# Loading and turning a mixer's input in halves, behind the last two hidden tiles of the mixer before it

## The chip, the cores and the metric

The kernel runs on one core of one Trainium2 chip. The metric is the device time of one execution in microseconds; the number compared is the median over several runs. TensorE (PE, its weight loads are listed as PEld), VectorE (DVE), ScalarE (ACT) and GpSimd (POOL) each work through their own list of instructions in order. SyncE (SP) issues the DMAs, also in order, so a DMA that must wait holds up every DMA behind it in that list.

## The reference

Linear attention per head, followed by a mixer over tokens and channels; everything is float32.

```
phi(x):  proj = x @ w_phi;  proj -= max(|proj|)           # per token, 64 -> 128
         return concat(exp(proj), exp(-proj))             # 256 features
q_p, k_p = phi(q), phi(k)                                 # q, k, v: 8 batches, 8 heads, 576 tokens, 64
kv, z = k_p^T @ v, sum over tokens of k_p
attn  = (q_p @ kv) / (q_p . z + 1e-6)                     # x: 8 x 576 x 512 after the heads are joined
u   = x + V^T (U^T x)          # over tokens, rank 32
out = u + relu(u @ w_ch1) @ w_ch2                         # 512 -> 2048 -> 512
```

The weights of the mixer (U, V, w_ch1, w_ch2) arrive as float64 and are converted on the chip.

## The kernel before, in words

**Attention.** Work goes through 32 pairs of heads, `Pair(b, j)` with batch b = 0 to 7 and j = 0 to 3. At a time there are three pairs in flight: `cur`, `nxt` and `far`. A pair's steps are `transposes` (k and q brought to features-on-partitions as tiles `T`), `s_project_k0` and `s_project_k1` (PSUM tiles `pkt` and `pk`, features `kp`), `s_project_q0` and `q1` (`pq`, `qp`), `s_kv` (`kv_ps`, copied by VectorE to `kv`), and `s_out` (`xpt`, `xp`, then `normalize` on VectorE, whose last multiplication writes `x`). From batch 2 on (`split`), k and q are loaded as 32 x 32 blocks into `raw`, and VectorE turns each block in place (STREAM_TRANSPOSE, line 347) before ScalarE and VectorE split it into a high and a low part.

**Tokens.** `tokens(tk, fill)` runs after the last pair of a batch: `split`, `down` (`pp`, then `pst` by ScalarE and VectorE), `up(t)` for t = 0 to 4 (TensorE writes `vp`, VectorE adds it to `x` or to `xt`, SyncE stores the result to the DRAM buffer `u_dram`). Five tiles cover the 576 tokens; the fifth, of 64 tokens, goes to a ninth row block that is mixed at the very end. `fill` holds the steps of the next batch's first pair, which are put between.

**Mixer.** `Mixer(g, x)` does relu(u @ w1) @ w2 for 512 tokens in 16 hidden tiles: `hidden(f)` is 12 matmuls into `ph`, which ScalarE turns into `h_hi` and VectorE into `h_lo` (line 667); `add(f)` is 12 matmuls that accumulate `h_hi` and `h_lo` times w2 into four PSUM tiles `o`. The right-hand side of `hidden` is `uT_hi` and `uT_lo`, one buffer each. From batch 2 on these come from `y`: `load_blocks` reads `u_dram` back in 32 x 32 blocks with four DMAs, and `turn_blocks(c)` turns a quarter on VectorE (line 653) and splits it (lines 258 and 259). `finish` adds the residual `st` to `o` on VectorE (line 704).

**Order.** The pieces of a mixer wait in the list `todo` (`chunks()`: hidden 0, hidden 1, add 0, hidden 2, add 1, ...). `pace.step()` after each attention step takes pieces from it, so that a mixer of batch b-1 is worked off among the attention steps of batch b. From pair 9 on TensorE's instructions keep the order in which they are written (`in_order`); on the other engines, and in SyncE's list, a scheduler sets the order from its own estimate, except where `tc.issue_after` puts an instruction behind a named one in the order (it adds no wait). At the end of `tokens` all but `HELD` = 4 pieces of the old mixer are emitted, then the new input is turned with two more pieces between, and the last two adds are left for the next steps.

**Names used below.** I call the stretch around the change of mixers a boundary; there are six, at the end of the tokens of batches 2 to 7. PSUM tiles of the tag `at` (`pkt`, `pk`, `pq`, `kv_ps`, `xpt`, `xp`, `vp`, `pp`) share three banks; `ph` has one bank, so `hidden(f + 1)` cannot begin before `h_lo` of tile f has been read out of it (but for the last mixers, which use `at` banks for every second `ph`).

## Time and profile before

| | |
|---|---|
| median of three runs | 1186.46 us (1184.69 to 1186.94) |
| the profiled execution | 1189.84 us, of which the span from first to last instruction is 1188.1 us |
| TensorE matmuls busy | 1130.9 us, 95% of the span, mean granted clock 0.982 |
| VectorE busy | 671.6 us, 57% |
| ScalarE busy | 538.9 us, 45% |
| GpSimd busy | 202.5 us, 17% |
| DMA moved | 110.28 MB, mean 93 GB/s |

Rows of the profile give an engine, a line of kernel.py, an operation, its output and inputs, its duration, and in square brackets the time that the engine stood idle just before it and what ended that wait. SPq is SyncE's list of DMAs: its duration is the time to issue, not the time to land. PEclk is the clock that TensorE was granted, as a share of full speed.

### The profile page before, as it was taken

What the parts mean: (1) busy time and instruction counts of PE and PEld (TensorE: products, weight loads), DVE (VectorE), ACT (ScalarE), POOL (GpSimd) and SP (SyncE); (2) the same over time, 40 slices, a digit from 0 to 9 for tenths busy, and PEclk for the clock granted to TensorE, in tenths of its full rate; (3) what the DMA queues carried; (4) which work ended last, traced back from release to release, by engine and by line L of the source; (5) the groups of instructions that cost most, each with busy time, mean ns of one, the idle gap of its engine ahead of it and who ended that gap; (6) DMA issues with size and microseconds to landing.
All of it is one profiled execution on the core that took longest, in us unless ns stands there. A gap on an engine that the chain in (4) does not pass through costs nothing.

```text
span 1188.1 us, 22127 instructions
## 1 busy us (share of the span) xinstructions
PE 1130.9 (95%) x8841; PEld 932.3 (78%) x8845; DVE 671.6 (57%) x1482; ACT 538.9 (45%) x1151; POOL 202.5 (17%) x154
## 2 busy tenths in 40 slices
PE   7989988999998999899999999899989998999998
PEld 5767866778887888688878888688878877888886
DVE  6567787766666666566657665666666433212111
ACT  6678887545444554254535544355535421111110
POOL 4234355211110111011201111011201200000000
PEclk9998999999999999899999999899999999999999
DMA  5785511332354224532363235323461117410201
GB/s 147 230 258 195 159 49 29 105 102 67 85 104 104 67 58 100 105 81 52 86 121 102 66 84 112 95 59 67 104 118 46 42 68 143 108 54 36 71 1 36
DMA packets 246599, 110.28 MB, mean 93 GB/s; under 512 B 211296, under 2 KB 223840, under 8 KB 246496
## 3 DMA queue, kind: packets, MB, share of 16 engines
q1 hardware_dynamic: 246176, 108.34, 36.5%
q8 instruction: 70, 1.15, 0.4%
q10 hardware_dynamic: 320, 0.52, 0.1%
q14 instruction: 33, 0.27, 0.1%
HBM read 86.80 MB, written 22.02 MB: 92 GB/s over the span
## 4 chain that ended last, share of the span: by engine, by line
PE 69%; DVE 13%; DMA 8%; SPq 4%; ACT 4%; issue 2%; POOL 1%; DVEq 0%; ACTq 0%; POOLq 0%
PE ph L79 26%; PE o L79 25%; PE kv_ps L79 5%; PE xp L79 4%; DMA y<-u_dram 3%; PE pq L79 2%; DMA raw<-in_k_dram 2%; PE pk L79 2%; SPq L647 2%; DVE T L351 1%; PE pp L79 1%; DMA u_dram<-x 1%; SPq L291 1%; DVE w L250 1%; DVE y L653 1%
## 5 line engine op out<-in xcount | busy, mean ns | idle before, releaser
L79 PE MATMUL ph<-uT_hi,w 128*128 128x512 f32 x1152 | 389.1, 399 | 11.2 <-DVE h_lo L667 9.6
L79 PE MATMUL o<-w,h_hi 128*128 128x512 f32 x1152 | 361.2, 399 | 0.4 <-ACT h_hi L666 0.3
L79 PEld LDWEIGHTS ph<-uT_hi,w 128*128 128x128 f32 x1152 | 218.9, 190 | 63.1 <-DVE h_lo L667 14.3
L79 PEld LDWEIGHTS o<-w,h_hi 128*128 128x128 f32 x1152 | 216.5, 191 | 46.4 <-ACT h_hi L666 1.9
L79 PE MATMUL o<-w,h_lo 128*128 128x512 f32 x576 | 226.4, 401 | 15.3 <-DVE h_lo L667 15.3
L79 PE MATMUL ph<-uT_lo,w 128*128 128x512 f32 x576 | 227.5, 395 | 3.5 <-DVE uT_lo L259 3.5
L666 ACT ACTIVATE h_hi<-ph 128x512 fp32r<-128x512 f32 x144 | 85.6, 595 | 294.6 <-PE ph L79 294.3
L667 DVE SCALAR_TENSOR_TENSOR h_lo<-ph,h_hi 128x512 fp32r<-128x512 f32 x144 | 98.9, 687 | 193.7 <-ACT h_hi L666 193.1
L395 POOL PARTITION_ALL_REDUCE qp<-qp x64 | 127.6, 1994 | 261.4 <-ACT qp L394 229.9
L79 PEld LDWEIGHTS o<-w,h_lo 128*128 128x128 f32 x576 | 110.8, 193 | 41.7 <-DVE h_lo L667 17.8
L79 PEld LDWEIGHTS ph<-uT_lo,w 128*128 128x128 f32 x576 | 109.7, 190 | 25.0 <-DVE uT_lo L259 4.2
L395 POOL PARTITION_ALL_REDUCE qp_t<-qp_t x32 | 25.1, 786 | 417.0 <-ACT qp_t L394 417.0
L79 PE MATMUL xp<-kv,qp 128*64 128x65 f32 x2048 | 72.3, 225 | 9.9 <-ACT qp L397 7.7
L351 DVE TENSOR_TENSOR T<-raw,T 64x512 fp32r<-64x512 f32 x96 | 67.7, 705 | 24.2 <-ACT T L350 21.9
L397 ACT ACTIVATE qp<-qp 128x512 f32<-128x512 f32 x64 | 40.3, 629 | 88.7 <-DVE qp L396 88.7
L79 PEld LDWEIGHTS xp<-kv,qp 128*64 128x64 f32 x2048 | 66.0, 140 | 17.3 <-ACT qp L397 9.6
L79 PE MATMUL kv_ps<-vb,kp 128*64 128x65 f32 x2048 | 70.4, 224 | 0.1
L79 PEld LDWEIGHTS kv_ps<-vb,kp 128*64 128x64 f32 x2048 | 64.0, 137 | 7.2 <-issue 2.4
L347 DVE STREAM_TRANSPOSE raw<-raw 128x512 f32<-128x512 f32 x48 | 34.1, 711 | 55.8 <-DMA raw<-in_k_dram 35.7
L385 ACT ACTIVATE kp<-kp 128x512 f32<-128x512 f32 x64 | 40.4, 632 | 54.5 <-DVE kp L382 54.4
L350 ACT CAST T<-raw 64x512 fp32r<-64x512 f32 x96 | 59.2, 617 | 8.7 <-PE pq L79 7.3
L396 DVE TENSOR_TENSOR qp<-qp 128x512 f32<-128x512 f32 x64 | 46.4, 725 | 14.7 <-POOL qp L395 14.5
(119 smaller groups left out, 1267.2 us busy)
## 6 DMA issues: line engine op xcount, KB each, us to landing
w<-kept SPq DMA_DIRECT2D x46, 512.0 KB, 3.8
words<-in_moe_w_ch_dram SPq DMA_DIRECT2D x32, 512.0 KB, 7.8
vb<-in_v_dram SPq DMA_DIRECT2D x64, 128.0 KB, 2.9
u_dram<-x SPq DMA_DIRECT2D x32, 256.0 KB, 2.5
st<-u_dram SPq DMA_DIRECT2D x16, 512.0 KB, 4.5
out_dram<-st SPq DMA_DIRECT2D x32, 256.0 KB, 2.2
y<-u_dram SPq DMA_DIRECT2D x28, 256.0 KB, 5.6
raw<-in_k_dram SPq DMA_DIRECT2D x96, 64.0 KB, 2.4
```

What stands on the lines that cost most here:

```text
L79: ins = nc.tensor.matmul(*args, **kw)
L250: nc.vector.tensor_sub(w[:, 1, :], r, f32(w[:, 0, :]))
L347: nc.vector.transpose(out=x_, in_=x_)
L350: nc.scalar.copy(out=m[here, s, :], in_=x_[here])
L351: nc.vector.tensor_sub(m[there, s, :], x_[here], f32(m[here, s, :]))
L385: nc.scalar.activation(out=kp[:, :, 0:F], in_=kp[:, :, F:2 * F], func=AF.Exp)
L395: nc.gpsimd.partition_all_reduce(qp[:, 0, :], qp[:, 1, :], P, ReduceOp.absmax)
L396: nc.vector.tensor_sub(qp[:, 1, :], qp[:, 1, :], qp[:, 0, :])
L397: nc.scalar.activation(out=qp[:, 0, :], in_=qp[:, 1, :], func=AF.Exp)
L647: nc.sync.dma_start(out=self.y[i * Q:(i + 1) * Q].rearrange("r c (j e) -> r c j e", e=Q), in_=of[i])
L666: on_act = nc.scalar.activation(out=h_hi, in_=ph, func=AF.Relu)
L667: on_dve = nc.vector.scalar_tensor_tensor(out=h_lo, in0=ph, scalar=0.0, in1=f32(h_hi), op0=ALU.max, op1=ALU.subtract)
```

## The change

Four things change.

1. `load_blocks(half)` loads `y` in two halves of 256 tokens, four DMAs each. The first half is loaded after `up(0)` and `up(1)`, the second after `up(2)` and `up(3)`. `turn_blocks(prev)` puts the turns of the first half behind `h_lo` of the old mixer's tile 14 and those of the second half behind `h_lo` of tile 15 in the order; the split into `uT_hi` and `uT_lo` follows the second half, in pieces of the old size. A new `last_chunks` emits all but two pieces of the old mixer, then the turns.
2. In `tokens` from batch 2 on, one pacing step ahead of `up(0)` is left out, so that each `up` stands one or two pieces earlier, and the next batch's second pair has its `s_project_k0` (as the last item of `fill`) ahead of hidden tile 14, rather than behind tile 15.
3. The in-place turns of `raw` stand behind the last multiplication of `normalize` (`divided`).
4. In the last batch, where there is no next pair, two pacing steps are taken ahead of `s_out`; ahead of the mixer of the ninth row block, all but seven pieces are emitted instead of all but four.

```diff
@@ Pair
-            self.raw = []
+            self.raw, self.kp0 = [], None
...
-                    nc.vector.transpose(out=x_, in_=x_)
+                    with tc.issue_after(divided[0].ins):
+                        nc.vector.transpose(out=x_, in_=x_)
@@ normalize
-            nc.vector.tensor_tensor(
+            divided[0] = nc.vector.tensor_tensor(
                 out=xo, in0=xv[:, :, 0:D], in1=den.unsqueeze(2).broadcast_to([np_, m, D]),
                 op=ALU.mult)
@@ Mixer
-        def load_blocks(self):
-            self.y = home.tile([P, NCC, SM], F32, tag="w_late", name=f"y{self.g}")
-            of = u_dram[self.g].rearrange("(j r) (c i e) -> i r c j e", r=Q, i=4, e=Q)
+        def load_blocks(self, half):
+            if half == 0:
+                self.y = home.tile([P, 2, NCC, SM // 2], F32, tag="w_late", name=f"y{self.g}")
+            ts_ = slice(half * SM // 2, (half + 1) * SM // 2)
+            of = u_dram[self.g][ts_].rearrange("(j r) (c i e) -> i r c j e", r=Q, i=4, e=Q)
             for i in range(4):
                 nc.sync.dma_start(
-                    out=self.y[i * Q:(i + 1) * Q].rearrange("r c (j e) -> r c j e", e=Q),
+                    out=self.y[i * Q:(i + 1) * Q, half].rearrange("r c (j e) -> r c j e", e=Q),
                     in_=of[i])
-        def turn_blocks(self, c):
-            y = self.y[:, c, :]
-            nc.vector.transpose(out=y, in_=y)
-            split_t(y, self.uT_hi[:, c, :], self.uT_lo[:, c, :])
+        def turn_blocks(self, prev):
+            for half in range(2):
+                with ExitStack() as order:
+                    for i in prev.parts[NFC - 2 + half]:
+                        order.enter_context(tc.issue_after(i.ins))
+                    for c in range(NCC):
+                        y = self.y[:, half, c, :]
+                        nc.vector.transpose(out=y, in_=y)
+                    if half:
+                        for c in range(NCC):
+                            split_t(self.y[:, :, c, :], *(
+                                a[:, c, :].rearrange("p (h n) -> p h n", h=2)
+                                for a in (self.uT_hi, self.uT_lo)))
@@ hidden
-            self.h[f] = (h_hi, h_lo)
+            self.h[f], self.parts[f] = (h_hi, h_lo), (on_act, on_dve)
@@ tokens
-        pace.step()
+        if not tk.late:
+            pace.step()
         tk.up(0)
         tk.up(1)
         if tk.late:
+            m = Mixer(tk.b, tk.x)
+            m.load_blocks(0)
             pace.step()
             tk.up(2)
             tk.up(3)
-            m = Mixer(tk.b, tk.x)
-            m.load_blocks()
+            m.load_blocks(1)
             pace.step()
             tk.up(NT)
-            mix(len(todo) - HELD)
-            for c in range(NCC):
-                m.turn_blocks(c)
-                mix(c % 2)
-            todo.extend(m.chunks())
+            mix(len(todo) - 5)
+            other()
+            last_chunks(m)
             return
...
+    def last_chunks(m):
+        prev = todo[0][0].__self__
+        mix(len(todo) - 2)
+        m.turn_blocks(prev)
+        todo.extend(m.chunks())
@@ the loop over pairs
-                step(nxt.s_project_k0)
+                if nxt.kp0 is None:
+                    nxt.s_project_k0()
+                pace.step()
                 if nxt.split:
                     pace.step()
+            else:
+                pace.step()
+                pace.step()
...
-                    if not nxt.split:
-                        fill.append(nxt.s_project_q1)
+                    fill.append(
+                        far.s_project_k0 if tk.late else
+                        None if nxt.split else nxt.s_project_q1)
+                    fill = [fn for fn in fill if fn is not None]
@@ the end
-        mix(len(todo) - HELD)
+        mix(len(todo) - 7)
...
-        m.load_blocks()
-        for c in range(NCC):
-            m.turn_blocks(c)
-            mix()
-        todo.extend(m.chunks())
+        m.load_blocks(0)
+        m.load_blocks(1)
+        last_chunks(m)
         mix(len(todo))
```

How that moves the instructions shows at three places of the boundary at the end of batch 2's tokens (and alike at those of batches 3 to 6). First VectorE, from the old mixer's tile 13 to the read-out of its sums (`mk`, `kp`: the key features of the next batch's second pair; `st`: the residual plus `o`). Before:

```order
514 L667 SCALAR_TENSOR_TENSOR h_lo_13_4103<-ph_13_4089,h_hi_13_4102 128x512
515 L347 STREAM_TRANSPOSE raw_3_4507<-raw_3_4507 128x512
516 L617 TENSOR_TENSOR xt_2826<-xt_2826,vp_4_4133 64x512
517 L667 SCALAR_TENSOR_TENSOR h_lo_14_4151<-ph_14_4137,h_hi_14_4150 128x512
518 L653 STREAM_TRANSPOSE y_4116<-y_4116 128x512 x4
519 L380 TENSOR_REDUCE mk_1_t<-pkt_1_4213 128x1
520 L667 SCALAR_TENSOR_TENSOR h_lo_15_4192<-ph_15_4178,h_hi_15_4191 128x512
521 L435 TENSOR_TENSOR kp_1_0_4222<-pk_3_1_4223,kp_1_0_4222 128x2x128
522 L435 TENSOR_TENSOR kp_1_0_4222<-pk_3_1_4228,kp_1_0_4222 128x2x128
523 L259 TENSOR_TENSOR uT_lo_4115<-y_4116,uT_hi_4114 128x512 x3
```

The same engine and place in the changed kernel:

```order
511 L436 TENSOR_TENSOR kp_1_0_4150<-pk_3_1_4151,kp_1_0_4150 128x2x128
512 L436 TENSOR_TENSOR kp_1_0_4150<-pk_3_1_4156,kp_1_0_4150 128x2x128
513 L381 TENSOR_REDUCE mk_1_0_4161<-kp_1_0_4150 128x4
514 L383 TENSOR_TENSOR kp_1_0_4150<-kp_1_0_4150,mk_1_0_4161 128x4x128
515 L680 SCALAR_TENSOR_TENSOR h_lo_14_4180<-ph_14_4166,h_hi_14_4179 128x512
516 L662 STREAM_TRANSPOSE y_4079<-y_4079 128x256 x4
517 L680 SCALAR_TENSOR_TENSOR h_lo_15_4209<-ph_15_4195,h_hi_15_4208 128x512
518 L662 STREAM_TRANSPOSE y_4079<-y_4079 128x256 x4
519 L259 TENSOR_TENSOR uT_lo_4078<-y_4079,uT_hi_4077 128x512 x2
520 L717 TENSOR_TENSOR st_0_4019<-st_0_4019,o_0_3036 128x512
```

Ahead of `h_lo_15` there are now only the four short turns of the first half; the key features have moved in front of `h_lo_14`.

Then VectorE a little later, where the outputs of the next batch's first pair are divided and the new mixer's first `h_lo` follows, in the changed kernel (before, the two turns of `raw` stood elsewhere, and `h_lo_0` came right behind the multiplication):

```order
536 L494 TENSOR_TENSOR x_4228<-xp_3_0_4291,den_0_0_4308 128x4x64
537 L494 TENSOR_TENSOR x_4228<-xp_3_0_4312,den_0_1_4329 128x4x64
538 L348 STREAM_TRANSPOSE raw_2_0_4229<-raw_2_0_4229 128x512
539 L348 STREAM_TRANSPOSE raw_2_1_4234<-raw_2_1_4234 128x512
540 L680 SCALAR_TENSOR_TENSOR h_lo_0_4347<-ph_0_4333,h_hi_0_4346 128x512
```

Two turns now stand between the last multiplication and the new mixer's first `h_lo`.

Last TensorE at the beginning of the boundary, where the second projection of q (`pq`) precedes the first two `up` tiles (`vp`) and add 11 of the old mixer (`o`); - is before, + the changed kernel:

```order
 L79 MATMUL pq_3_0_4060<-T_3_0_3663,w_hl 128x512 x2
+L79 MATMUL vp_0_4069<-pst_3368,v_all 128x512
+L79 MATMUL vp_1_4073<-pst_3368,v_all 128x512
 L79 MATMUL o_0_3036<-w_11_2231,h_hi_11_3907 128x512 x2
 L79 MATMUL o_0_3036<-w_11_2231,h_lo_11_3908 128x512
@@ -825,17 +827,16 @@
 L79 MATMUL o_3_3039<-w_11_2231,h_hi_11_3907 128x512 x2
 L79 MATMUL o_3_3039<-w_11_2231,h_lo_11_3908 128x512
-L79 MATMUL vp_0_4081<-pst_3368,v_all 128x512
-L79 MATMUL vp_1_4085<-pst_3368,v_all 128x512
```

The two `vp` matmuls have moved from behind the twelve of add 11 to right behind `pq`. In SyncE's list the four loads of `y` have become two groups of four, the first ahead of the last stores of `u_dram`, the second behind them and behind four of the eight loads of `raw`. In the last batch the outputs of the last pair (`xpt`, `xp`) have moved on TensorE from between hidden 9 and add 8 to between hidden 10 and add 9, and `pp` there is followed by `vp` at once, where hidden 11 stood between.

More of the change, by code (lines that the diff above doesn't have):

```diff
@@ L262, in tile_kernel @@
     SPLIT, Q, H = 2, 32, P // 2
-    tails = {}
+    tails, divided = {}, [None]
     class Pair:
@@ L627, in __init__ @@
             self.uT_lo = moe.tile([P, NCC, 512], F32R, tag="uT_lo", name=f"uT_lo{g}")
-            self.o, self.h, self.res = None, {}, None
+            self.o, self.h, self.parts, self.res = None, {}, {}, None
         def transposes(self, t):
```

## The prediction

> **What bounds the kernel now.** I read the page's busy shares first, then what TensorE waited for, then TensorE, VectorE and SyncE in order of time around one boundary, and at last the granted clock in ten microseconds around each boundary.
>
> ```profile
> PE 1130.9 (95%) x8841; PEld 932.3 (78%) x8845; DVE 671.6 (57%) x1482; ACT 538.9 (45%) x1151; POOL 202.5 (17%) x154
> ...
> PE o L79 <- DVE h_lo L667: 15.3, 6, 3.5
> PE ph L79 <- DVE h_lo L667: 9.6, 10, 2.6
> ...
> DVE y L653 <- DMA y<-u_dram: 45.5, 7, 7.4
> ```
>
> TensorE is the bound: 1130.9 of 1188.1 us. The columns of the waits are total, count and longest. So a change of order can win back what TensorE stands idle, and the clock that it loses by that. Few long waits make most of it, and they are for `h_lo`, which VectorE makes. Why VectorE is late shows at the boundary of batch 3 (TensorE first, then VectorE, then SyncE):
>
> ```profile
> 489.64 0.61 PE L79 MATMUL o<-w,h_hi 128*128 128x512 f32 x2
> 493.75 0.80 PE L79 MATMUL o<-w,h_lo 128*128 128x512 f32 x1 [3.50 <-DVE h_lo L667]
> ...
> 481.58 0.69 DVE L667 SCALAR_TENSOR_TENSOR h_lo<-ph,h_hi 128x512 fp32r<-128x512 f32 x1 [2.05 <-ACT h_hi L666]
> 489.66 2.49 DVE L653 STREAM_TRANSPOSE y<-y 128x512 f32<-128x512 f32 x4 [7.38 <-DMA y<-u_dram]
> 493.00 0.69 DVE L667 SCALAR_TENSOR_TENSOR h_lo<-ph,h_hi 128x512 fp32r<-128x512 f32 x1
> 494.27 1.89 DVE L259 TENSOR_TENSOR uT_lo<-y,uT_hi 128x512 fp32r<-128x512 f32 x3
> 498.07 1.88 DVE L704 TENSOR_TENSOR st<-st,o 128x512 f32<-128x512 f32 x3
> 502.15 0.76 DVE L493 TENSOR_TENSOR x<-xp,den 128x256 f32<-128x256 f32 x2
> 504.81 0.69 DVE L667 SCALAR_TENSOR_TENSOR h_lo<-ph,h_hi 128x512 fp32r<-128x512 f32 x1 [1.91 <-ACT h_hi L666]
> ...
> 476.67 0.94 SPq L620 DMA_DIRECT2D u_dram<-x  x2
> 479.46 6.62 SPq L647 DMA_DIRECT2D y<-u_dram  x4
> 486.18 1.30 SPq L620 DMA_DIRECT2D u_dram<-xt  x1
> ```
>
> VectorE stands 7.38 us in front of the turns of `y`, whose loads were issued at 479.46 and had landed at 489.66; the last `h_lo` of the old mixer is queued behind them, and TensorE waits 3.50 us for it. The other boundaries read alike; at the last one the wait is booked on `ph` (2.64, below). What the wait costs beyond itself shows in the granted clock (PEclk, third from the end of a row):
>
> ```profile
> 364.00:374.00 10.00, 8.64 (x99) 6.87 (x100) 9.78 (x27) 3.18 (x7) 0.00 (x0) 1.00 0.33 121
> 493.00:503.00 10.00, 9.25 (x90) 7.49 (x91) 9.68 (x26) 1.88 (x4) 0.00 (x0) 0.67 0.28 105
> 622.00:632.00 10.00, 9.93 (x100) 8.12 (x100) 8.99 (x26) 2.43 (x6) 0.00 (x0) 0.83 0.29 107
> 750.00:760.00 10.00, 10.00 (x94) 8.03 (x95) 8.92 (x25) 1.88 (x4) 0.00 (x0) 0.72 0.29 107
> 878.00:888.00 10.00, 9.63 (x98) 8.00 (x99) 9.29 (x26) 2.32 (x6) 0.00 (x0) 0.83 0.29 107
> 997.00:1007.00 10.00, 8.79 (x29) 6.55 (x30) 4.05 (x8) 2.68 (x5) 0.00 (x0) 0.83 0.11 43
> 957.00:967.00 10.00, 7.38 (x57) 6.05 (x52) 4.85 (x17) 2.89 (x7) 0.00 (x0) 0.83 0.03 9
> ```
>
> Five of six boundaries run at 0.67 to 0.83 of full speed for the ten microseconds after the wait. The seventh row is the last pair of batch 7, where TensorE waits for q's features.
>
> **What the change takes away.** (a) The turns leave their place in front of `h_lo`. The `o` group's six waits are 15.3 us, and the row of 997.82 below adds 2.64: 17.9 us.
>
> ```profile
> 997.82 0.77 PE L79 MATMUL ph<-uT_hi,w 128*128 128x512 f32 x1 [2.64 <-DVE h_lo L667]
> 364.62 0.50 PE L79 MATMUL o<-w,h_lo 128*128 128x512 f32 x1 [2.78 <-DVE h_lo L667]
> 622.07 0.52 PE L79 MATMUL o<-w,h_lo 128*128 128x512 f32 x1 [2.54 <-DVE h_lo L667]
> ...
> 477.90 0.50 PE L79 MATMUL ph<-uT_hi,w 128*128 128x512 f32 x1 [1.31 <-DVE h_lo L667]
> 607.15 0.50 PE L79 MATMUL ph<-uT_hi,w 128*128 128x512 f32 x1 [0.28 <-DVE h_lo L667]
> 863.37 0.50 PE L79 MATMUL ph<-uT_hi,w 128*128 128x512 f32 x1 [0.37 <-DVE h_lo L667]
> ...
> 959.43 0.34 PE L79 MATMUL xp<-kv,qp 128*64 128x65 f32 x4 [2.29 <-ACT qp L397]
> 960.09 1.61 PE L79 MATMUL xp<-kv,qp 128*64 128x65 f32 x28 [0.33 <-ACT qp L398]
> ```
>
> (b) The clock behind those waits. Ten microseconds times one minus the clock is 3.3, 1.7, 2.8, 1.7 and 1.7 us; at the boundary of batch 3 some 0.4 of it falls into the wait itself. 10.8 us. (c) The three waits at 477.90, 607.15 and 863.37, where a turn of `raw` that waits for its DMA stands ahead of `h_lo`: 2.0 us. (d) In the last batch hidden 10 and add 8 now run while q's features are made; twelve matmuls of either kind are 2.7 us by the chain of waits:
>
> ```profile
> 508.69 2.74 PE o L79 x12
> ```
>
> So the waits of 2.29 and 0.33 go, and the clock of the seventh row, 1.7: 4.3 us. Sum 35.0 us.
>
> Of the clock the Trainium skill says, in "TensorE: Matmul & The Clock Gate", section "HAM oscillation — how this bites in real kernels", that idle gaps longer than about 3.4 us are to be avoided. By that sentence alone the shorter waits here would cost no clock. The trace does not agree: 2.54 us of idle at 622.07 brought a clock of 0.83, though 2.78 at 364.62 brought none.
>
> **What it adds.** Three prices, and two that I set to nothing. (e) The first two `vp` come right behind `pq`. The second needs the bank of `kv_ps`, which VectorE must have copied out:
>
> ```profile
> 466.54 0.73 PE L79 MATMUL pq<-T,w_hl 128*128 128x512 f32 x2
> 469.85 0.62 PE L79 MATMUL vp<-pst,v_all 128*128 128x512 f32 x2
> ...
> 466.46 0.42 DVE L602 TENSOR_TENSOR pst<-pp,pst 32x256 fp32r<-32x256 f32 x1
> 467.63 0.43 DVE L484 COPY kv<-kv_ps 128x260 f32<-128x260 f32 x1
> ```
>
> `pq` ends at 467.27, so TensorE would reach that `vp` at about 467.3, and the copy ends at 468.06: at least 0.7 us. The turns of `raw` now stand ahead of the splits of `x` and add up to 1.0 us to VectorE's lateness: at most 1.7. I take 1.2 at five boundaries, 6.0 us (3.5 to 8.5). A gain is excluded, since no wait stood there. At the last boundary `vp` follows `pp` directly, and the way over ScalarE and VectorE shows:
>
> ```profile
> 972.30 0.37 ACT L601 CAST pst<-pp 128x256 fp32r<-128x256 f32 x1 [3.32 <-PE pp L79]
> 972.70 0.42 DVE L602 TENSOR_TENSOR pst<-pp,pst 32x256 fp32r<-32x256 f32 x1 [3.00 <-ACT pst L601]
> ```
>
> Together 0.8, with hand-overs 0.9 us. (f) VectorE behind the last `h_lo`. By the rows above it has 0.6 for `h_lo`, four short turns (half of 2.49, so 1.3), four `uT_lo` (0.63 each by 1.89 for three, 2.5), four `st` (2.5), the divisions (from 499.95, where `st` ends, to 502.91, less one key-feature step that has moved, as long as an `h_lo`: 2.4), and two turns of `raw` (as long as two of the four of 2.49: 1.3): 10.6 us, begun 0.7 after the old mixer's last `ph`. TensorE does two adds (2.7 each), `xpt` and `xp` (2.3) and hidden 0 (2.7), then 0.6 for the next `pk`, 11.0 us. The new `h_lo` would end at 11.9 and let TensorE go on at 12.0: a wait of 1.0 to 1.4, against this before:
>
> ```profile
> 505.55 0.50 PE L79 MATMUL ph<-uT_hi,w 128*128 128x512 f32 x1 [0.76 <-DVE h_lo L667]
> ```
>
> So 0.6 more per boundary; with the second half's loads perhaps late (below) I take 0.8, at five boundaries 4.0 us (0 to 7). (g) Moving the key projection ahead of hidden 14 costs nothing: its VectorE work, 2.7 us, falls into the 7.38 that were idle. (h) The instructions are four more DMAs and four more turns per boundary, but the same elements.
>
> The loads are what can spoil it. Count from the second `vp`. The adds and stores of x end at 2.4, and the first load follows 1.85 later (476.67 + 0.94 to 479.46), at 4.3. The whole `y`, 1 MB, took 10.2 us from first issue to the first turn; half takes 5.1 if it goes by bytes, 8.4 at worst (half the issue time plus the full 3.6 behind the last issue, and 1.5 for other loads on the queue). First half landed at 9.4 to 12.7. It is needed when `h_lo_14` is done, 12.2 (add 11, `vp`, hidden 13, add 12, `pk`, hidden 14) plus 1.4: 13.6. It is in time. The second half is issued behind the first (4.3 + 3.3), two stores of x (0.94), one of xt (1.30) and four of `raw`:
>
> ```profile
> 470.91 1.92 SPq L291 DMA_DIRECT2D raw<-in_k_dram  x4
> ```
>
> With 1.9 for those it is issued from 11.7 on and landed at 16.8 to 20.1, needed at 19.1 (`h_lo_15`). That is on the edge, and likelier in time, since the bytes of the trace's own 10.2 us give the early end.
>
> Of small transfers the Trainium skill says, in "DMA: Bandwidth & Descriptors", section "Anatomy of one DMA — SWDGE (gpsimd) path", that each DMA pays about 2.0 us whatever its size, which speaks against halves. If that added up, four more would make the second half 8 us later. Four loads of 256 KB in 10.2 us would leave room for such a price, but no trace here shows a load of 128 KB of this kind.
>
> **Sum.** 35.0 - 6.0 - 0.9 - 4.0 = 24.1 us. The profiled execution took 1189.84 us, so 1165.7; it lies 3.4 above the median of the three runs, 1186.46, and against that the forecast is 1162.4 us. Batches 0 and 1, where the scheduler's order changes too, I leave at 0, plus or minus 3.
>
> **Rivals.** *New waits that lose clock* (1175, range 1170 to 1180): if (e) or (f) comes to 2.5 us, the clock rows return, 1.7 us at each of five boundaries, and with both terms at their dear ends (8.5 and 7) the gain is 35.0 - 8.5 - 0.9 - 7 - 8.5 = 10 us, some 1176. For it: (f) is VectorE without a pause for 10 us. Against: 1.31 us of idle at 477.90 brought no lower clock.
> *The clock is not bought by these waits* (1173): if (b) stays, 24.1 - 10.8. For it: 2.78 us at 364.62 lost none. Against: the other five did. (The 3.4 us of the Trainium skill's clock page would give this case.)
> *Slower*: the second half lands L late, and VectorE, which stands in front of it, holds `uT`, the divisions and the new `h_lo`. It decides from about L = 2.7: five times L, plus 1.7 to 2.9 of clock at each, eats 24 us. At L = 5, 5 x 5 + 5 x 2.3 = 36, so 1199. For it: the estimate is on the edge. Against: that needs a landing at 21.8, beyond my late end of 20.1. (The fixed price in the Trainium skill's DMA page, if it added up, would give this case.)
> *It does not do what it says* (1186): that `h_lo_15` stays late for the first half's turns. Against: 13.6 against 9.4 to 12.7.
> *Better* (1152): no lateness in (e) and (f), 35.0 - 3.5 - 0.9 = 30.6, and 3 in the early batches.
>
> **How the numbers follow.** Forecast case 1156 to 1169: 0.60. New waits: 0.18. Clock stays: 0.06. Better: 0.08. No change: 0.03. Slower: 0.05. The early batches' 3 us blur the edges. The range, 1153 to 1177, leaves out no change, slower and the ends of two others, together below 0.2. Within 0.2% (2.4 us, about what repeated runs of this kernel can tell from no change) 0.03, slower 0.05, faster 0.92.
>
> **What would show it.** The page's waits: `o` for `h_lo` under 2 us in place of 15.3; no VectorE wait for `y`, or one under 2 us each; five waits of `vp` for `kv` of 0.7 to 1.7; `ph` behind the new mixer's first tile waiting 1.0 to 1.8. Clock 1.00 in the ten microseconds around each boundary. I am wrong if VectorE waits long for the second half, or if TensorE's clock falls behind the new waits.

## The result, and the profile after

The changed kernel takes 1151.58 us (median of four runs, 1151.45 to 1152.33), the kernel before on the same chip 1186.7 us: a ratio of 0.970, interval 0.967 to 0.973. The gain of 35.1 us is 11.0 more than the forecast's 24.1, and the time lies 1.4 us under the low end of the range. The profiled execution took 1151.47 us, with a span of 1149.7. One run each of two experiments below took far longer than the rest (1383.64 and 3851.92 us) and is left out of their medians.

From the page of the kernel after: the busy shares, the two waits of TensorE that the change leaves or makes (total, count, longest), and the issues of `y` (count, size, median from issue to landing).

```profile
PE 1117.7 (97%) x8841; PEld 928.0 (81%) x8845; DVE 675.5 (59%) x1510; ACT 539.6 (47%) x1151; POOL 204.2 (18%) x154
...
PE ph L79 <- DVE h_lo L680: 5.5, 6, 1.5
...
PE vp L79 <- DVE pst L603: 0.9, 1, 0.9
...
y<-u_dram SPq DMA_DIRECT2D x56, 128.0 KB, 3.7
```

The group `o` for `h_lo` (15.3 us) is gone, and so is VectorE's wait for `y` (45.5 us). The boundary of batch 3 in the kernel after, in order of time (SyncE, then VectorE, then TensorE):

```profile
466.47 2.79 SPq L650 DMA_DIRECT2D y<-u_dram  x4
473.70 3.69 SPq L650 DMA_DIRECT2D y<-u_dram  x4
...
481.20 0.69 DVE L680 SCALAR_TENSOR_TENSOR h_lo<-ph,h_hi 128x512 fp32r<-128x512 f32 x1 [2.82 <-ACT h_hi L679]
481.81 1.42 DVE L662 STREAM_TRANSPOSE y<-y 128x256 f32<-128x256 f32 x4
490.38 1.29 DVE L348 STREAM_TRANSPOSE raw<-raw 128x512 f32<-128x512 f32 x2
491.84 0.69 DVE L680 SCALAR_TENSOR_TENSOR h_lo<-ph,h_hi 128x512 fp32r<-128x512 f32 x1 [0.17 <-ACT h_hi L679]
...
492.59 0.50 PE L79 MATMUL ph<-uT_hi,w 128*128 128x512 f32 x1 [0.77 <-DVE h_lo L680]
```

`h_lo_15` now waits for ScalarE alone, the turns of the second half start without a wait, and of the whole boundary TensorE has one wait left, 0.77 us. Ten microseconds around each of the five boundaries, with the granted clock third from the end (it is 1.00 around the last boundary too):

```profile
361.00:371.00 10.00, 9.18 (x105) 7.66 (x104) 9.48 (x26) 3.17 (x8) 0.00 (x0) 1.00 0.37 134
483.00:493.00 10.00, 9.23 (x106) 7.70 (x105) 9.57 (x26) 3.23 (x8) 0.00 (x0) 1.00 0.34 125
605.00:615.00 10.00, 9.18 (x106) 7.64 (x104) 9.52 (x26) 3.19 (x8) 0.00 (x0) 1.00 0.32 115
728.00:738.00 10.00, 9.23 (x105) 7.73 (x104) 9.54 (x26) 3.23 (x8) 0.00 (x0) 1.00 0.38 138
850.00:860.00 10.00, 9.18 (x105) 7.67 (x104) 9.51 (x26) 3.17 (x8) 0.00 (x0) 1.00 0.37 134
```

**A finer ruler.** The copies `kv<-kv_ps` on VectorE come at fixed places of the program, so the time between two of them prices one stretch. The table has the five intervals that hold a boundary (batches 2 to 6), the end (from the last copy to the end of the span) and the start (up to the copy before the first boundary), in us, from the one profiled execution of each kernel. The names of the experiments are explained below.

| kernel | start | 2 | 3 | 4 | 5 | 6 | five together | end |
|---|---|---|---|---|---|---|---|---|
| before | 339.4 | 46.5 | 49.5 | 47.5 | 49.0 | 47.6 | 240.1 | 235.6 |
| after | 339.4 | 42.5 | 42.4 | 42.5 | 42.5 | 42.5 | 212.5 | 226.8 |
| after, once more | 340.1 | 42.5 | 42.4 | 42.5 | 42.9 | 42.5 | 212.9 | 226.7 |
| after, last batch's steps out | 339.9 | 42.5 | 42.4 | 42.5 | 42.5 | 42.5 | 212.5 | 231.2 |
| after, raw turns undone | 341.1 | 43.3 | 42.4 | 43.9 | 43.2 | 43.3 | 216.1 | 226.6 |
| after, key projection undone | 337.2 | 43.4 | 43.4 | 43.5 | 43.4 | 43.4 | 217.1 | 226.7 |
| after, halves undone | 338.3 | 43.3 | 44.0 | 43.9 | 43.2 | 43.3 | 217.7 | 226.7 |
| after, both of these undone | 340.5 | 44.4 | 49.0 | 44.3 | 48.6 | 44.6 | 230.9 | 226.8 |
| before, turns moved | 339.6 | 46.4 | 48.7 | 46.6 | 48.7 | 47.4 | 237.7 | 228.8 |
| before, turns moved, store earlier | 341.1 | 47.1 | 47.5 | 47.1 | 46.2 | 46.4 | 234.4 | 228.6 |
| before, raw turns moved | 337.2 | 47.9 | 49.0 | 49.2 | 48.1 | 46.8 | 241.0 | 236.9 |
| after, five extra `h_lo` | 338.0 | 46.2 | 46.2 | 45.9 | 45.8 | 45.8 | 230.0 | 226.6 |
| after, eight extra `h_lo` | 340.3 | 49.3 | 49.5 | 48.3 | 48.5 | 49.6 | 245.1 | 226.7 |
| after, two more moves | 337.2 | 42.6 | 42.5 | 42.6 | 43.0 | 42.6 | 213.3 | 225.5 |

Kernels with the same instructions up to that point differ by up to 2.9 us at the start (337.2 and 340.1, at a granted clock of 0.99 and 0.97 up to there), while an interval that nothing touches repeats within 0.1 us, once 0.5. So single prices are read from the table and not from the medians. Between before and after the boundaries give 27.6 us, the end 8.8, and batch 3's own steps another 1.9 (its two intervals up to the boundary); the start gives nothing in these two executions (339.45 and 339.37).

### The profile page after: what moved, and what is told of

The parts are those of the page before. It is cut to its first block, busy times and chain, and to the rows that moved or that the text cites. A ratio compares the mean times of both kernels' runs of the same rounds, so it can differ in the third digit from the quotient of the medians.

```text
span 1149.7 us, 22209 instructions
## 1 busy us (share of the span) xinstructions
PE 1117.7 (97%) x8841; PEld 928.0 (81%) x8845; DVE 675.5 (59%) x1510; ACT 539.6 (47%) x1151; POOL 204.2 (18%) x154
## 3 DMA queue, kind: packets, MB, share of 16 engines
q8 instruction: 70, 1.15, 0.4%
## 4 chain that ended last, share of the span: by engine, by line
PE 86%; DVE 7%; ACT 4%; issue 1%; POOL 0%; SPq 0%; DMA 0%; DVEq 0%; ACTq 0%; POOLq 0%
PE ph L79 32%; PE o L79 32%; PE kv_ps L79 6%; PE xp L79 5%; PE pk L79 3%; PE pq L79 3%; PE pp L79 1%; DVE w L250 1%; PE xpt L79 1%; PE vp L79 1%; ACT w_ab L148 1%; ACT w_ab L147 1%; DVE w_ab L151 1%; PE T L83 1%; DVE qp L397 1%
## 5 line engine op out<-in xcount | busy, mean ns | idle before, releaser
L79 PE MATMUL o<-w,h_hi 128*128 128x512 f32 x1152 | 355.4, 393 | 0.7 <-ACT h_hi L679 0.6
L79 PEld LDWEIGHTS o<-w,h_hi 128*128 128x128 f32 x1152 | 213.2, 188 | 45.7 <-ACT h_hi L679 1.5
L79 PE MATMUL ph<-uT_lo,w 128*128 128x512 f32 x576 | 226.7, 394 | 3.4 <-DVE uT_lo L259 3.4
L79 PE MATMUL o<-w,h_lo 128*128 128x512 f32 x576 | 221.9, 393 | 0.0
L79 PEld LDWEIGHTS ph<-uT_lo,w 128*128 128x128 f32 x576 | 109.0, 189 | 25.2 <-DVE uT_lo L259 4.0
L79 PEld LDWEIGHTS o<-w,h_lo 128*128 128x128 f32 x576 | 108.5, 189 | 23.0
L397 DVE TENSOR_TENSOR qp<-qp 128x512 f32<-128x512 f32 x64 | 47.9, 749 | 17.3 <-POOL qp L396 16.8
L435 ACT COPY kp<-pk 128x256 f32<-128x256 f32 x96 | 31.3, 377 | 54.2 <-PE pk L79 54.2
```

Source lines behind the costliest of these rows:

```text
L79: ins = nc.tensor.matmul(*args, **kw)
L397: nc.vector.tensor_sub(qp[:, 1, :], qp[:, 1, :], qp[:, 0, :])
L435: nc.scalar.copy(out=kp[:, ts_, 0:F], in_=pk[:, :, 1, :])
```

## The experiments

**Raw turns undone in the kernel after.**

```
-                    with tc.issue_after(divided[0].ins):
-                        nc.vector.transpose(out=x_, in_=x_)
+                    nc.vector.transpose(out=x_, in_=x_)
```

> The change with its raw-turn part undone: the raw turns may stand ahead of the division again. Theory A (the forecast's term (e), the second vp waiting 1.2 us for the copy of kv_ps, was priced at a boundary where VectorE was late because a raw turn had waited 4.17 us for its load, and the change itself takes that wait away): the raw turns wait for their loads again, the copy of kv_ps starts 0.5 to 1.5 us behind the end of kv_ps at one boundary or more and TensorE's vp waits there; with the 2.0 us of part (c) that is 1153 to 1159 us. Rival B (the copy is on time whatever the raw turns do, because less of VectorE's other work stands ahead of it now): no vp wait but that of 0.9 for pst, and at most the 2.0 us of part (c) come back, 1151.5 to 1153.5.

Measured 1156.79 us (1154.82 to 1159.17), ratio 0.973 (0.970 to 0.976). VectorE and TensorE in that kernel:

```profile
450.98 0.71 DVE L347 STREAM_TRANSPOSE raw<-raw 128x512 f32<-128x512 f32 x1 [4.66 <-DMA raw<-in_q_dram]
...
452.33 0.50 PE L79 MATMUL ph<-uT_hi,w 128*128 128x512 f32 x1 [1.23 <-DVE den_t L491]
467.26 0.50 PE L79 MATMUL vp<-pst,v_all 128*128 128x512 f32 x1 [0.58 <-DVE kv L484]
```

Theory A holds. The turn waits 4.66 us for its load, and 16 us later the second `vp` waits 0.58 us for the copy: the very wait that I had priced, at the very boundary where I had read the price. It is the only one; at the other four boundaries `vp` waits for nothing even here. The rest is waits of the kind of part (c): 1.23 us at 452.33, and 0.46, 1.12, 0.43 and 0.57 of `ph` for `h_lo` at the other four boundaries. The part is worth 6.1 us in this company (3.6 at the boundaries, 2.5 in batch 3), not 2.0. That is read from the slowest of the four executions (1159.17); the others are 1.1 to 4.4 us shorter, so the size is less sure than the sign.

**The key projection back at its old place.**

```
-                        far.s_project_k0 if tk.late else
                         None if nxt.split else nxt.s_project_q1)
```

> The change with K's first projection left at its old place, behind Q's and ahead of the output stage of the next step, not in the fill ahead of the last projection of the mixer. Theory A (what keeps TensorE fed at a boundary while ScalarE and VectorE finish the last tile and the halves is the stretch of projections between, and the K projection is 5 of the roughly 11 us that the chain h_lo of tile 15, second turns, four pairs of splits takes): the first ph of the new batch waits some 2 to 5 us instead of 0.8 at five boundaries, most of them long enough to cost clock, 1165 to 1185 us. Rival B (the order on TensorE does not matter there since other chunks stand in its place): within 2 us of 1151.6.

Measured 1154.2 us (1153.73 to 1154.91), ratio 0.971 (0.968 to 0.974). At each of the five boundaries 0.9 us more, 4.6 in all. The sign is A's, the size is not: the wait of `ph` grows by half a microsecond only, and the clock stays at 1.00.

```profile
492.17 0.50 PE L79 MATMUL ph<-uT_hi,w 128*128 128x512 f32 x1 [1.28 <-DVE h_lo L680]
```

On VectorE the way from `h_lo_15` to the end of the division of `xt` is 8.48 us at batch 5 in the kernel after and 10.32 here, since four steps of key features stand in it; half of the 1.84 us was slack.

**The halves undone:** four loads of 256 KB where the second half was asked for, four turns of 128x512 behind `h_lo_15`.

```
-            for half in range(2):
+            with ExitStack() as order:
...
-                    for i in prev.parts[NFC - 2 + half]:
+                    for i in prev.parts[NFC - 1]:
```

> The change with y loaded whole (four loads of 256 KB, issued where the second half is) and turned whole behind the last tile's h_lo, all else as in the change. Four turns of 128x512 at 0.67 us stand behind the last h_lo instead of four of 128x256 at 0.40: 1.1 us more. Theory A (the halves are needed: the chain behind the last h_lo has no slack, its end is what ph waits 0.8 us for): ph waits 0.8 + 1.1 = 1.9 us at six boundaries, 1158 us, with clock lost at some of them up to 1168. Theory A2 (the whole load lands later than its turn can start, 4 loads of 256 KB being issued in about 4 x 0.7 us and landing some 6 us after the last): another 1 to 3 us on top, up to 1175. Rival B (placement alone counts, the halves only move what was hidden): 1151.6 within 1.5 us.

Measured 1155.65 us (1155.22 to 1156.59), ratio 0.972 (0.969 to 0.975). Theory A's 1.1 us per boundary comes out as 0.8 to 1.6, 5.2 together, at five boundaries and without loss of clock (`ph` waits 1.28, not 1.9); A2's late landing does not happen: one turn in the whole run waits 0.5 us for its load. The turns themselves are 2.48 us for four against 1.42 for the second half.

**The last batch without its two pacing steps.** (The expectation calls them steps of projection; they are two calls of `pace.step()`, which give TensorE a hidden tile and an add of the old mixer.)

```
             else:
-                pace.step()
-                pace.step()
```

> The change with the two steps of projection taken out of the last batch's path (the added else branch with no next batch), so that the output stage of batch 7 stands directly behind its attention. By the forecast's term (d): the pair of waits of 2.29 and 0.33 us and 1.7 us of lower clock come back, 4.3 us less the 0.0 that the steps cost where they stand: 1155.9 us. Rival: the two steps were worth only their listed waits, 2.6 us and no clock, 1154.2; or the last batch's waits have other causes and nothing comes back, 1151.6.

Measured 1156.91 us (1156.4 to 1157.4), ratio 0.973 (0.970 to 0.977). The end is 4.4 us longer; part (d) said 4.3. The pair of waits, of which the first is shown, and the lower clock are back in this kernel:

```profile
930.39 0.34 PE L79 MATMUL xp<-kv,qp 128*64 128x65 f32 x4 [2.29 <-ACT qp L398]
...
930.50:940.50 10.00, 9.67 (x63) 8.07 (x64) 3.10 (x9) 2.73 (x7) 0.00 (x0) 0.83 0.16 54
```

**The kernel before with the turns moved, and nothing else:** four whole turns behind `h_lo_15`, then the splits.

```
+            prev = todo[0][0].__self__
+            mix(len(todo) - 2)
+            m.turn_blocks(prev)
```

> The kernel before with one thing done: y is loaded whole as before, but its four turns stand behind the h_lo of the old mixer's last tile (with the splits), not ahead of the last HELD chunks; no halves, K's first projection where it was, raw turns where they were, the paces where they were. Theory A (the placement of the turns behind h_lo_15 alone carries the 28.7 us of the forecast's parts (a) and (b)): the six waits of o for h_lo and their clock go, against them stand what the two undone parts were worth in the kernel after, 1.1 + 0.9 us per boundary for whole turns and K's late projection and the waits of raw turns: a gain of 15 to 25 us, 1162 to 1172. Rival B (the placement only moves the wait of TensorE from o to ph of the new batch, since the uT chain begins later by all of the turns and K's projection is not there to cover it): ph waits 2 to 4 us at each boundary and loses clock, a gain under 8 us, 1179 to 1187.

Measured 1181.29 us (median of nine, 1179.82 to 1186.42), ratio 0.995 (0.993 to 0.997): rival B, but that the wait is not where it put it. The end gains 6.8 us, the other five boundaries 2.4 together. TensorE's wait has moved from `o` not to `ph` but to `pk`, 2.7 to 2.9 us at all five, and clock is lost at each. Batch 4 and then batch 5 in this kernel:

```profile
616.77 2.49 DVE L657 STREAM_TRANSPOSE y<-y 128x512 f32<-128x512 f32 x4 [1.82 <-DMA y<-u_dram]
627.60 1.21 PE L79 MATMUL pk<-w_hl,T 128*128 128x256 f32 x4 [2.71 <-DVE xt L493]
...
732.98 5.63 SPq L647 DMA_DIRECT2D y<-u_dram  x4
738.71 1.77 SPq L620 DMA_DIRECT2D u_dram<-xt  x1
743.60 0.48 DVE L937 MEMSET xt<- 64x512 f32 x1 [3.45 <-DMA u_dram<-xt]
744.32 0.68 DVE L672 SCALAR_TENSOR_TENSOR h_lo<-ph,h_hi 128x512 fp32r<-128x512 f32 x1
745.06 0.50 PE L79 MATMUL o<-w,h_lo 128*128 128x512 f32 x1 [1.51 <-DVE h_lo L672]
```

At batch 4 the load of `y` is still late for the turns by 1.82 us. At batches 3 and 5 something else shows that I had not read: the `MEMSET` that clears `xt` for the next pair of batches stands ahead of `h_lo_15`, and waits for the store of the old `xt`, which is queued on SyncE behind all four loads of `y`.

**The same, with the loads of `y` asked for after that store.**

```
-            m.load_blocks()
             pace.step()
             tk.up(NT)
+            m.load_blocks()
```

> The kernel before with the turns behind h_lo_15, as in the run with that part alone, and one more step: the loads of y are asked for after the store of the last token tile (xt to u_dram), so that this store stands on SyncE behind one load of y and not behind all four. Theory A (in the run with the turns alone, VectorE's MEMSET of xt stood ahead of h_lo_15 and waited 3.45 us for that store, which was queued behind 5.6 us of y loads; so o waited 1.51 us for h_lo_15, and the chain behind it ran late): the MEMSET waits under 1 us ahead of h_lo_15 or not at all, o waits 0 for h_lo_15, and pk's wait for xt falls from 2.7 to 1.1 to 1.9 us; with the clock windows that the smaller waits no longer cost, 1.5 to 3.2 us less at five boundaries: 8 to 16 us, 1165 to 1173. Rival (the chain from the turns to xt is what TensorE waits for, and the wait of 1.51 us only moves to pk): within 3 us of 1181.

Measured 1178.49 us (1177.64 to 1179.61), ratio 0.992 (0.989 to 0.995). The wait of `o` is gone, and most of the time is not: the rival (within 3 us of 1181), if only just. The ruler gives 3.3 us at the five boundaries.

```profile
736.85 1.17 SPq L620 DMA_DIRECT2D u_dram<-xt  x1
738.06 3.72 SPq L647 DMA_DIRECT2D y<-u_dram  x3
740.59 0.48 DVE L937 MEMSET xt<- 64x512 f32 x1 [1.59 <-DMA u_dram<-xt]
746.16 2.49 DVE L657 STREAM_TRANSPOSE y<-y 128x512 f32<-128x512 f32 x4 [1.65 <-DMA y<-u_dram]
756.98 0.36 PE L79 MATMUL pk<-w_hl,T 128*128 128x256 f32 x1 [2.52 <-DVE xt L493]
```

The store was in front of three loads now, so the turns waited for those instead. Theory A was also wrong to expect it at five boundaries: the `MEMSET` comes at two (batches 3 and 5), which gain 1.2 and 2.5 us; the others move by 0.5 to 1.0, two up and one down.

**Halves and key projection both undone in the kernel after** (the last two edits on the kernel after, together).

> The kernel after with both parts undone that cost 4.6 and 5.2 us at the five boundaries when undone singly: y whole, and K's first projection at its old place. The raw turns stay behind the division. The chain from h_lo_15 to the end of xt's division was 8.48 us on VectorE with the change, 10.32 without K's projection ahead, 9.54 without the halves, 11.27 in the run with the turns alone. Theory A (VectorE's chain sets it, and each microsecond past the slack of 1.33 us ahead of pk is a wait): the chain is 11.4 us, pk waits 1.4 to 1.7 us for xt, the first ph of the new tile another 0.8, so 2 to 2.5 us per boundary against the kernel after, 10 to 13 us, 1162 to 1165, unless the MEMSET of xt holds h_lo_15 again; if it does, 20 to 25 us, 1172 to 1177. Rival (the two parts cover for one another): 5 to 6 us as with one, 1157.

Measured 1170.5 us (1168.16 to 1171.82), ratio 0.985 (0.982 to 0.988). At batches 2, 4 and 6 1.8 to 2.1 us are added, nearly as Theory A has it; at 3 and 5 6.6 and 6.2, where the `MEMSET` is and the clock falls too (0.66 from 750 to 760). The total lies between Theory A's two cases. Batch 4, then batch 5 in this kernel:

```profile
613.00 2.48 DVE L661 STREAM_TRANSPOSE y<-y 128x512 f32<-128x512 f32 x4
623.81 0.93 PE L79 MATMUL pk<-w_hl,T 128*128 128x256 f32 x4 [0.79 <-DVE xt L494]
...
737.09 0.48 DVE L955 MEMSET xt<- 64x512 f32 x1 [5.42 <-DMA u_dram<-xt]
749.54 0.93 PE L79 MATMUL pk<-w_hl,T 128*128 128x256 f32 x4 [2.42 <-DVE xt L494]
```

Undone singly the two cost 4.6 and 5.2 us, undone together 18.4. The `MEMSET` shows why. With the halves undone alone, the store of `xt` stands behind all four loads too, and the `MEMSET` waits 3.46 us for it; but with the key projection ahead, the old mixer's tiles come later against it (the store is issued 0.3 us ahead of `h_lo_14`, with both undone 0.9 us behind it), and `h_lo_15` still waits for ScalarE when the `MEMSET` is done. Batch 5 in that kernel:

```profile
727.37 0.48 DVE L956 MEMSET xt<- 64x512 f32 x1 [3.46 <-DMA u_dram<-xt]
728.48 0.69 DVE L676 SCALAR_TENSOR_TENSOR h_lo<-ph,h_hi 128x512 fp32r<-128x512 f32 x1 [0.63 <-ACT h_hi L675]
```

With the key projection undone alone, the store goes out between the two groups of loads, and the `MEMSET`, which waits 4.19 us there, is done before `h_lo_14`, for which TensorE does not wait. So either part keeps the `MEMSET` out of the way of `h_lo_15`; with both undone it holds it.

At batch 4 the turns need not wait for the load, as they did with the turns alone; `pk` waits 0.79 us here and 2.71 there, and that difference of 1.92 is close to the 1.82 of the load. So a third part seems to count: with `vp` right behind `pq` and the raw turns out of the way, the stores of x and with them the loads of `y` go out earlier (9.8 us behind the start of `pq` instead of 12.3). That last step is read from the traces of two kernels which differ in more than this, and was not tried alone.

**The kernel before with only the raw turns moved.**

```
-                    nc.vector.transpose(out=x_, in_=x_)
+                    with tc.issue_after(divided[0].ins):
+                        nc.vector.transpose(out=x_, in_=x_)
```

> The kernel before with only the raw turns put behind the division. By the forecast's part (c): the waits of 1.31, 0.28 and 0.37 and a further one of 0.70 us go, 2.0 to 2.7 us faster, 1184.5 to 1185. Theory A (the raw turn's wait for its load held VectorE, which made the copy of kv late at the boundary of batch 3): the copy of kv at the boundary of batch 3 starts on time, within 0.1 us of the end of kv_ps; the gain may be up to the 6 us that undoing the part cost in the kernel after, 1181. Rival: the 6 us there came about only with the halves in place, and 2 us or less are seen here, 1184.5 to 1187.

Measured 1190.46 us (median of nine), ratio 1.001 (0.999 to 1.003). The copy of `kv_ps` at batch 3 is on time, as Theory A says, and nothing is gained:

```profile
464.89 0.43 DVE L485 COPY kv<-kv_ps 128x260 f32<-128x260 f32 x1
487.02 2.49 DVE L654 STREAM_TRANSPOSE y<-y 128x512 f32<-128x512 f32 x4 [8.13 <-DMA y<-u_dram]
491.12 0.50 PE L79 MATMUL o<-w,h_lo 128*128 128x512 f32 x1 [4.25 <-DVE h_lo L668]
```

VectorE reaches the turns of `y` earlier and waits 8.13 us there instead of 7.38, and TensorE's wait for `h_lo` grows from 3.50 to 4.25. Batch 3's own steps gain 1.8 us by the same copies, and the boundaries and the end lose 2.2. So what the part wins in front of a wait for a transfer was worth nothing here, and some 6 us once that wait was gone.

**A late second half, imitated in the kernel after:** the `h_lo` of tile 15 is computed five, and eight, more times at five boundaries, to the same values.

```
+            for _ in range(5 if f == NFC - 1 and 1 <= self.g <= 5 else 0):
+                on_dve = nc.vector.scalar_tensor_tensor(...)
```

> The kernel after with the h_lo of tile 15 computed five more times at each of five boundaries (same values), which delays all that stands behind it on VectorE by about 5 x 0.65 = 3.3 us: a stand-in for a second half that comes late by L = 3.3. About 1.7 us of slack stand behind h_lo_15 for the splits. Theory A (a late uT is paid as a wait of ph, clock is lost only if one window of 3.4 us holds more than about 1.7 us of idle): ph waits 1.6 to 2.4 us at five boundaries, in all 8 to 12 us and clock at none or some, 1160 to 1168. Rival (the forecast's: L costs in full and each such wait loses 1.7 to 2.9 us of clock): 5 x 3.3 + 5 x 2.3 = 28 us, 1180.

> As with five, but eight more times: L = 8 x 0.65 = 5.2 us. Theory A: ph waits 3.5 to 4.3 us at five boundaries, which is over 1.7 us in one window of 3.4 us, so the clock is halved for one or two windows behind each, 1.7 to 3.4 us more: 26 to 38 us in all, 1178 to 1190. Rival 1 (as the forecast's slower case): 5 x 5.2 + 5 x 2.3 = 37 us, 1189. Rival 2 (a wait alone costs no clock): 18 to 21 us, 1171.

Measured 1168.47 us (1167.52 to 1168.88), ratio 0.983 (0.981 to 0.986), and 1184.23 us (median of ten), ratio 0.997 (0.995 to 0.998). Five:

```profile
736.10 3.59 DVE L683 SCALAR_TENSOR_TENSOR h_lo<-ph,h_hi 128x512 fp32r<-128x512 f32 x5
739.75 0.50 PE L79 MATMUL o<-w,h_lo 128*128 128x512 f32 x1 [1.87 <-DVE h_lo L683]
750.10 0.50 PE L79 MATMUL ph<-uT_hi,w 128*128 128x512 f32 x1 [1.29 <-DVE h_lo L680]
```

3.59 us of delay cost 3.3 to 3.4 us where the clock stays (batches 4 to 6) and 3.7 to 3.8 where it falls (2 and 3). Theory A was too cheap with five (17.5 together, not 8 to 12), since the delay is paid in two places, at `o` and at `ph`, and the chain has only 0.2 to 0.3 us to spare. The forecast's rule (all of L, and 1.7 to 2.9 of clock besides) was too dear: TensorE at half clock comes later to the next wait, and finds it shorter (0.82 and 0.77 instead of 1.29 at batches 2 and 3). With eight, 5.77 us of delay cost 5.8 to 7.1, 32.6 together, inside Theory A's 26 to 38, where the forecast's rule gives 40 for that delay; the long wait, 4.04 us, is at `o` and not at `ph`, and clock is lost at all five. By this run the slower rival would have needed a lateness of about 6 us, and not of 2.7, to eat the gain that came about.

**Two more moves on the kernel after:** a pacing step between the halves of the first pair's output stage (again a piece of the mixer, and no projection), and the step ahead of `up(0)` back for the last batch.

```
+                cur.out_main(0, cur.qp0, x)
+                pace.step()
+                cur.out_main(1, cur.qp1, x)
...
-        if not tk.late:
+        if not tk.late or tk.b == B - 1:
             pace.step()
```

> The kernel after with two more moves: one step of the projection between the two halves of the first pair's output stage, so that TensorE has work where ph waits 0.8 us for h_lo at five boundaries, and the step ahead of up(0) restored for the last batch, where vp waits 0.92 us for pst. Theory: the five waits (0.8 + 0.16 each) go, 4.8 us, and the last one, 1.1 us: 1146 us, 5 to 6 us less than the kernel after. Rival 1: the ph is as late as before because VectorE's h_lo comes after the divisions, and the step only moves a wait: 1150.5 to 1151.5. Rival 2: the step taken there is missing later, and a wait of equal length opens where it stood: no change or 1 to 2 us worse.

> The changed kernel once more, as the standard for the run ahead of it on the same chip: 1151 to 1153 us.

Measured 1149.53 us (1148.88 to 1150.83), ratio 0.968 (0.965 to 0.970), and the changed kernel beside it 1150.09 us (1149.5 to 1152.56), ratio 0.968 (0.966 to 0.971): no difference. At the boundaries rival 2 is right. The wait of 0.77 to 0.82 is gone from `ph`, and another stands ahead of it in this kernel:

```profile
612.83 0.41 PE L79 MATMUL pqt<-tail_T,w_hl 128*128 128x128 f32 x2 [0.55 <-DVE x L494]
```

The second move wins 1.2 us at the end, which the medians can't tell.

## Why the prediction was too high

**(a), (b), (d): right.** The six waits and the clock behind them went, with nothing late in their place; (d) is 4.4 by its own experiment against 4.3. The sum of what is removed, 35.0 us, less the 0.9 at the last boundary, which came out as priced, is 34.1; the medians give 35.1. The spans of the two profiled executions, from which the prices were read, differ by 38.4, since that of the kernel before was a long one. TensorE's idle time in them falls by 25.2 us (1188.1 less 1130.9 to 1149.7 less 1117.7), where the forecast's terms without the clock give 21.6, and its busy time by 13.2, where the terms for the clock give 12.5. Of the idle time 1.44 us stand in rows that I left out (a wait of 0.70 at 453.17, and one of 0.74 of `pk` for `xt` at 373.12); the rest no wait lists: the row of four `pk` matmuls, say, is 0.93 us long at 373.12, and 0.64 where nothing is late.

By place, the forecast had 16.0 us for the five boundaries (26.0 taken away, 10.0 added by (e) and (f)) and 8.1 for the last boundary and the end; the table shows 27.6 and 8.8. So the miss is at the five boundaries, and most of it is what (e) and (f) were to add there.

**(e): the step that failed first.** 6.0 us for the second `vp` behind the copy of `kv_ps`; it is 0 at all five boundaries. The copy starts 0.04 to 0.09 us after the end of `kv_ps`, and `vp` behind `pq` without a wait:

```profile
459.57 2.09 PE L79 MATMUL kv_ps<-vb,kp 128*64 128x65 f32 x64
461.70 0.43 DVE L485 COPY kv<-kv_ps 128x260 f32<-128x260 f32 x1
462.16 0.63 PE L79 MATMUL vp<-pst,v_all 128*128 128x512 f32 x2
```

The 0.7 us were read at batch 3 of the kernel before, where VectorE was late because a raw turn had waited 4.17 us for its load, and that wait is what part (c) takes away. I took a price from a state that the change itself ends, and multiplied it by five without looking at another boundary: at batches 2, 4, 5 and 6 of the kernel before the copy was on time. The turn at batch 3 and the copy at batch 5, both of before:

```profile
451.83 0.71 DVE L347 STREAM_TRANSPOSE raw<-raw 128x512 f32<-128x512 f32 x1 [4.17 <-DMA raw<-in_q_dram]
...
724.20 0.43 DVE L484 COPY kv<-kv_ps 128x260 f32<-128x260 f32 x1 [0.93 <-PE kv_ps L79]
```

**(f): mis-sized, 0 for 4.0 us.** VectorE's chain is 10.5 us by the rows of batch 3 (481.20 to 491.67), as forecast (10.6), but TensorE's work beside it is 11.3 and not 11.0 (at batch 5 from 725.18, where the old mixer's last `ph` ends, to 736.46, where the wait begins), and the new `h_lo` starts 0.17 us after VectorE is free, when ScalarE has made `h_hi`. So the wait is 0.77, as before the change, where I had 1.0 to 1.4; the other parts of the 0.8 per boundary, the upper end of that range and 0.2 for late loads, were not needed. The five extra `h_lo` show how near it was: 0.2 to 0.3 us of slack.

**(c): right as a sum, wrong as a part.** Alone it gives nothing, in company some 6 us. **(g), (h):** (g) had no price where the key projection goes to, and that was right; but leaving it behind would have cost 4.6. The halves, which I had only checked for harm, are worth 5.2 us, and with the key projection 18.4. At batches 3 and 5 either of the two is enough to keep `h_lo_15` from waiting for the `MEMSET`: the halves let the store of `xt` out between two groups of loads, the key projection puts tile 15 later. With both, the `MEMSET` waits 1.03 us at batch 5, where with the turns moved alone it waits 3.45.

**The loads** were in time: the second half is issued 11.3 us behind the second `vp` (473.70 less 462.39) where I had 11.7. One load takes 3.7 us (median) from issue to landing, against 5.6 for one of twice the size. The fixed price of some 2.0 us for each DMA that the Trainium skill names ("DMA: Bandwidth & Descriptors", section "Anatomy of one DMA — SWDGE (gpsimd) path") is near what this pair gives, 1.8 (3.7 less the 1.9 that the second 128 KB take), but it did not add up over the loads, which overlap: the four issued from 473.70 on had landed by 481.81, in 8.1 us, where four times 3.7 would be 14.8.

**Better (1152)** was the rival that came true, and had 0.08. That its number is so near is luck in part: it still counted 3.5 us for (e), which was 0, and 3 us from the early batches, of which the table shows nothing. Half of its condition was one fact, VectorE's lateness at the copy, which further boundaries of the trace of before would have shown; the other half, (f), hung on 0.3 us of TensorE's work.

## What to carry to other kernels

When the price of a new wait is read from how late an engine is in the old trace, look first at why it was late there, and whether the change removes that reason; read it at every repetition of the loop and not at one. What a part is worth alone says little of its worth in company: here a gain in front of a wait for a transfer was lost, and behind it each part of a chain of queues (a load, a store behind it, a clear that waits for the store) could hold the same instruction. Price single parts from the time between two fixed points of the program, since the run's total moves by more than they do.

## What the runs showed of the clock

The forecast could not say why 2.54 us of idle cost clock and 2.78 did not. The five like waits of 1.87 us in the kernel with five extra `h_lo` show it: two cost clock, three did not. Stretches of that kernel, cut every 3.413 us from the start of a half-clock one; idle is 3.41 less TensorE's busy time, the first figure behind the comma:

```profile
359.72:363.13 3.41, 1.54 (x7) 1.05 (x6) 3.34 (x8) 0.91 (x2) 0.00 (x0) 1.00 0.02 5
363.13:366.55 3.42, 3.42 (x26) 2.45 (x26) 3.42 (x7) 1.27 (x3) 0.00 (x0) 0.50 0.41 153
486.02:489.43 3.41, 1.54 (x8) 1.24 (x7) 3.34 (x8) 1.16 (x3) 0.00 (x0) 1.00 0.00 0
489.43:492.84 3.41, 3.41 (x35) 2.56 (x35) 3.41 (x7) 1.02 (x2) 0.00 (x0) 0.50 0.41 154
612.30:615.71 3.41, 1.71 (x7) 1.42 (x8) 3.34 (x8) 1.38 (x3) 0.00 (x0) 1.00 0.00 0
615.71:619.13 3.42, 3.42 (x78) 2.90 (x77) 3.42 (x7) 0.81 (x2) 0.00 (x0) 1.00 0.43 158
```

And two stretches of the kernel before, cut the same way:

```profile
362.99:366.40 3.41, 1.78 (x8) 1.48 (x9) 3.41 (x9) 1.45 (x3) 0.00 (x0) 1.00 0.02 5
622.40:625.81 3.41, 3.41 (x10) 2.62 (x8) 3.41 (x8) 0.62 (x2) 0.00 (x0) 0.50 0.00 0
```

In the kernel with five extra `h_lo` the two stretches at half clock stand 126.30 us apart, 37 times 3.413. A stretch with 1.87 us idle is followed by one at half clock, one with 1.70 is not, and at the other two boundaries the grid cuts the wait so that no stretch has more than 1.14 and 1.36. So a wait costs clock by how it falls on this grid. In the kernel before, the 2.54 us at 622.07 lie whole in the stretch ahead of 622.40, where the half clock begins; 76 stretches earlier the grid falls on 362.99 and cuts the 2.78 us at 364.62 into 1.15 and 1.63. At its batches 3 and 5 the half clock lasts two stretches: the first of the two had 1.03 and 1.28 us idle itself.

The Trainium skill says, in "TensorE: Matmul & The Clock Gate", section "What's actually happening", that the window is 3413 ns long and free-running, and the runs agree. The Trainium skill's rule that gaps of over 3.4 us are to be avoided (same page, section "HAM oscillation — how this bites in real kernels") does not fit them: about half a window was enough. In the kernel with five extra `h_lo`, stretches with up to 1.70 us idle cost no clock. That is no sharp limit: with the turns moved alone a stretch with 1.46 us idle (from 754.37) is followed by half clock, and one with 1.86 (from 952.34) is not. What else counts besides the listed idle time, these runs do not show.
